# Retention and a Mish feed-forward on one core: all early loads in one order, and what their consumers need around them

## The chip, the core and the metric

The kernel runs on one core of a Trainium2 chip. A core has a matrix engine (TensorE, PE in the profile, with its weight loads as PEld), VectorE (DVE), ScalarE (ACT), GpSimd (POOL), SyncE (SP), and 16 DMA engines that move data between the device's memory (HBM) and the core's SBUF. Every engine works through its own list of instructions in order; semaphores tie the lists together. PE writes only to PSUM, from which VectorE and ScalarE read. DMA transfers are issued by SyncE, ScalarE or GpSimd, each with a queue of its own.

The metric is the time of one execution in device microseconds (us), less is better.

## The reference

Eight batches, eight heads, 576 positions, head size 64. The output of retention, heads side by side, is the input of a feed-forward layer with Mish:

```python
scores = (1/sqrt(64)) * q @ k^T
gamma  = 1 - 2 ** (-5 - h)                      # one per head h
Dmat   = gamma ** (i - j) where i >= j, else 0
x      = (scores * Dmat) @ v                     # (8*576, 512)
h      = x @ w_in                                # w_in (512, 2048)
g      = h * tanh(log(1 + exp(h)))               # Mish
out    = g @ w_out                               # w_out (2048, 512)
```

Inputs and output are float32; the kernel multiplies in bf16.

## The kernel before

**Tiles.** Positions are cut into chunks of 128 per batch (the last 64 of two batches make one chunk), 36 chunks in all, and four chunks are a tile of 512 rows: nine tiles. Tiles 0 and 1 hold the first chunk of each batch, 0 to 3 in tile 0 and 4 to 7 in tile 1. These need no state from earlier positions and have code of their own, the `f_` functions. The later tiles carry a state per batch (`state`, `step_o`). For each tile, `g1` makes one of 16 slices of h (four matmuls over w_in into the PSUM tile `hp`, then Mish by ScalarE into `gT`), and `g2` or, for tile 0, `g2_first` multiplies with w_out.

**Tiles 0 and 1.** `load_rows(queue, t, i, b)` loads q (i = 0) or k (i = 1) of one batch of tile t as float32, 256 KB, into `raw`, which lies in the two halves of a buffer (`stage`) that later is a `gT`. Tile 1's q takes the half that tile 0's k had and the other way round; tile 0's masked scores (`sm`) also lie in the half of its k. So tile 1's load of q of batch b may start only when the masked scores of batch b of tile 0 have been used by `f_out`, and its load of k when tile 0's q of that batch has been cast. `f_cast` casts to bf16, for one group of two batches or, with `one`, for one batch of it. `f_transpose` turns q and k of a group with 16 PE transposes into PSUM and copies them to `qT` and `kT`. `f_scores` makes the scores of a group (16 matmuls) and VectorE multiplies them with the decay (`sm`). `f_v` casts v of a batch; `f_out` multiplies `sm` with v and copies the result into `xT`, the input of g1.

**Order.** The program is written in the order in which each engine is to work (a manual schedule); an instruction's place among those of its engine is its place in the code. `keep_warm(n)` issues n matmuls on zeros whose result nobody reads. Tile 0's first g1 is done in two halves of the columns (`half`), the first as soon as batches 0 and 1 are ready.

**Queues.** SyncE issues six of tile 0's q and k loads and ScalarE two, before anything else (L114 to L117). GpSimd makes the constants and masks, then issues v of batches 0 and 1 (L112), then waits with a cast of v (L438) before w_in's first quarter (L439) and the v of batches 2 and 3, and so on; w_out follows at L465, then v of tile 1, then the loads of later chunks (`load`, three transfers each, and `load_k0`). Every load by GpSimd is marked by one of eight semaphores in turn, so that a load waits for the eighth before it to have landed. In g1's slices 6 and 12 of tile 0 a copy of a few values of `gT` (`passed`, L484) stands in SyncE's queue and behind it four loads of tile 1's q and k (L485), so that these are not issued before the Mish of that slice is done.

**Behind tile 0's g1** come the casts of tile 1's first group by VectorE (L487) and the 16 steps of `g2_first`; among them, by the table `steps`, tile 1's transposes (T), scores (S), casts of its second group (C), of its v (V), and its `f_out` (O). Then `g1` of tile 1 begins, with the chunks of the later tiles between its slices (`att`: P scales q, V scales v, T transposes, S scores, O output).

Of the kernel before, what the change touches and what calls it, by code (L numbers as in the profile page):

```python
# [11 lines left out]
BF16 = mybir.dt.bfloat16  # L12
AX = mybir.ActivationFunctionType
# [4 lines left out]
def kernel(  # L18
# [18 lines left out]
    nc = tc.nc  # L37
    B, H, S, D = q.shape
    assert (B, H, S, D) == (8, 8, 576, 64)
    P = 128  # L40
# [21 lines left out]
    consts = ctx.enter_context(tc.tile_pool(name="consts", bufs=1))  # L62
# [9 lines left out]
    ps_sc = ctx.enter_context(tc.tile_pool(name="ps_sc", bufs=2, space=PS))  # L72
    ps_st = ctx.enter_context(tc.tile_pool(name="ps_st", bufs=1, space=PS))
    ps_h = ctx.enter_context(tc.tile_pool(name="ps_h", bufs=2, space=PS))
    ps_o = ctx.enter_context(tc.tile_pool(name="ps_o", bufs=1, space=PS))
# [9 lines left out]
    def load_w_in(f0, n):  # L85
        nc.gpsimd.dma_start(out=w_in_t[:, :, ds(f0, n)], in_=w_in_r[:, :, ds(f0, n)])

    def load_w_out(i):
        nc.gpsimd.dma_start(out=w_out_t[:, ts(i, 4), :], in_=w_out_r[:, ts(i, 4), :])
# [11 lines left out]
    def load_rows(queue, t, i, b):  # L101
        queue.dma_start(out=raw[t][i][:, b, :],
                        in_=(q, k)[i][4 * t + b, :, 0:P, :].rearrange("h (g r) d -> g h (r d)", r=8))

    def load_second_qk(g):
        for b in (2 * g, 2 * g + 1):
            for i in range(2):
                load_rows(nc.sync, 1, i, b)

    def load_first_v(b):  # L110
        v0[b] = io.tile([P, H, D], F32, name="vraw", bufs=8)
        nc.gpsimd.dma_start(out=v0[b], in_=v[b, :, 0:P, :].rearrange("h p d -> p h d"))  # L112

    for i, b in ((0, 0), (0, 1), (0, 2), (1, 2), (0, 3), (1, 3)):  # L114
        load_rows(nc.sync, 0, i, b)
    for b in range(2):
        load_rows(nc.scalar, 0, 1, b)  # L117

# [2 lines left out]
    lnd = consts.tile([P, 1], F32)  # L121
# [6 lines left out]
    ident = consts.tile([P, P], BF16)  # L128
    make_identity(nc, ident)
    pos = consts.tile([P, 5], F32)  # L130
    nc.gpsimd.iota(pos, pattern=[[P, 5]], base=0, channel_multiplier=1,
                   allow_small_or_imprecise_dtypes=True)
    nc.gpsimd.iota(pos[64:P, 4:5], pattern=[[1, 1]], base=512, channel_multiplier=1,
                   allow_small_or_imprecise_dtypes=True)
    mask = consts.tile([P, P], F32)
    mask2 = consts.tile([P, P], F32)
    nc.gpsimd.memset(mask, 1.0)
# [16 lines left out]
    nc.scalar.activation(gq, ex, AX.Exp)  # L154
    nc.scalar.activation(gv, ex, AX.Exp, scale=-1.0)
    warm = consts.tile([P, 1], F32)

    diag = consts.tile([P, 2], F32)
    nc.vector.memset(diag, 0.0)
# [3 lines left out]
    def keep_warm(n, pool=ps_o, name="ops"):  # L163
        idle = pool.tile([P, 512], F32, name=name)
        for _ in range(n):
            nc.tensor.matmul(idle, lhsT=zeros[:, 0:P], rhs=zeros, start=True, stop=True)
# [5 lines left out]
    fst = {}  # L172
# [4 lines left out]
    def f_cast(t, i, g, copy, xs=slice(0, 2)):  # L177
        name = ("qb", "kb")[i]
        if t not in fst:
            fst[t] = {n: first.tile([P, 2, 8, 2, D], BF16, name=n) for n in ("qb", "kb")}  # L180
            fst[t]["vb"] = {}
        copy(fst[t][name][:, g, :, xs, :].rearrange("p r x d -> p x r d"),  # L182
             raw[t][i][:, ds(2 * g, 2), :][:, xs, :].rearrange("p x (r d) -> p x r d", r=8))

    def f_transpose(t, g, copies, tps):
        for i, name in enumerate(("qb", "kb")):
            for r in range(8):
                nc.tensor.transpose(tps[i][:, r, :], fst[t][name][:, g, r, :, :].rearrange("p x d -> p (x d)"),  # L188
                                    ident)
        for i, name in enumerate(("qb", "kb")):  # L190
            out_t = first.tile([P, H, P], BF16, name=name + "T", bufs=2)
            copies[i](out_t.rearrange("p h (g r) -> p h g r", r=8),
                      tps[i].rearrange("p r (g h) -> p h g r", h=H))
            fst[t][name, g] = out_t

    def f_scores(t, g):
        qT, kT = fst[t]["qb", g], fst[t]["kb", g]
# [14 lines left out]
    def f_v(t, b, copy):  # L212
        vb = first.tile([P, H, D], BF16, name="vb", bufs=4)
        copy(vb, v0[4 * t + b])
        fst[t]["vb"][b] = vb

    def f_out(t, b, copy):
        if b == 0:
            xts[t] = xp.tile([P, KC, NCH * P], BF16, name="xT")
        vb = fst[t]["vb"][b]  # L220
        if t == 0:
            pool, name = ((ps_h, "hp"), (ps_h, "hp"), (ps_st, "st"), (ps_o, "ops"))[b]
            ot = pool.tile([P, NP, P], F32, name=name)
        else:
            ot = ps_sc.tile([P, 2, NP, P], F32, name="sc")[:, 0]
        for p in range(NP):
            for e in range(2):
                nc.tensor.matmul(ot[ds(64 * e, 64), p, :], lhsT=vb[:, 2 * p + e, :],
                                 rhs=fst[t]["sm", b][:, 2 * p + e, :],
                                 start=(p == 0), stop=True, skip_group_check=True)  # L230
        copy(xts[t][:, :, ts(b, P)], ot)  # L231

    def f_state(t, b, engine=nc.gpsimd):

        n = 4 * t + b
        v0s[n] = first.tile([P, H, D], BF16, name="v0s", bufs=B)
        engine.tensor_tensor(v0s[n], v0[n], gv[:, 0, :].unsqueeze(2).to_broadcast([P, H, D]), op=OP.mult)
# [118 lines left out]
    gts = {}  # L356
    outs = {}

    def g1(t, f, cols=slice(0, NCH * P)):
        if t not in gts:  # L360
            gts[t] = gp.tile([P, nF, NCH * P], BF16, name="gT")
        hp = ps_h.tile([P, NCH * P], F32, name="hp")
        for c in range(KC):
            nc.tensor.matmul(hp[:, cols], lhsT=w_in_t[:, c, ts(f, P)], rhs=xts[t][:, c, cols],  # L364
                             start=(c == 0), stop=(c == KC - 1))
        nc.scalar.activation(gts[t][:, f, cols], hp[:, cols], AX.Mish)  # L366
# [62 lines left out]
    dve, act, pool = nc.vector.tensor_copy, nc.scalar.copy, nc.gpsimd.tensor_copy  # L429
# [1 line left out]

    half = (slice(0, 2 * P), slice(2 * P, 4 * P))
    one = (slice(0, 1), slice(1, 2))
    f_cast(0, 0, 0, dve, one[0])
    f_cast(0, 1, 0, dve, one[0])
    f_cast(0, 0, 0, dve, one[1])
    f_cast(0, 1, 0, act, one[1])
    f_v(0, 0, pool)  # L438
    load_w_in(0, 512)  # L439
    for b in (2, 3):  # L440
        load_first_v(b)
    f_v(0, 1, pool)
    for i in range(1, 4):
        load_w_in(512 * i, 512)
    keep_warm(11)
    f_transpose(0, 0, (act, dve), [ps_h.tile([P, 8, P], BF16, name="hp") for _ in range(2)])
    for i, x in ((0, 0), (0, 1), (1, 0), (1, 1)):
        f_cast(0, i, 1, act, one[x])
    keep_warm(3, ps_sc, "sc")
    f_scores(0, 0)  # L450
    f_transpose(0, 1, (act, act), [ps_st.tile([P, 8, P], BF16, name="st"), ps_o.tile([P, 8, P], BF16, name="ops")])
    f_out(0, 0, act)
    f_out(0, 1, dve)
    f_scores(0, 1)
    nc.scalar.activation(warm, pos[:, 0:1], AX.Mish)
    f_v(0, 2, pool)
    f_v(0, 3, act)
    for f in range(4):
        g1(0, f, half[0])
    f_out(0, 2, act)  # L460
    f_out(0, 3, dve)
    for f in range(4):
        g1(0, f, half[1])
    for i in range(4):
        load_w_out(i)  # L465
    for b in range(4):
        f_state(0, b)
    for b in range(4, 8):
        load_first_v(b)
    for b in range(4):  # L470
# [3 lines left out]
    nc.vector.tensor_scalar(gq, gq, 1.0 / math.sqrt(D), None, op0=OP.mult)  # L474

    passed = consts.tile([P, 2, 8], BF16)
    for f in range(4, nF):  # L480
        g1(0, f)
        if f in (6, 12):
            g = f // 6 - 1
            nc.sync.dma_start(out=passed[0:16, g, :], in_=gts[0][0:16, f, 0:8])  # L484
            load_second_qk(g)  # L485
    for i in range(2):
        f_cast(1, i, 0, dve)  # L487
    steps = {0: "T0", 3: "S0 C1", 9: "T1", 11: "S1", 12: "V0 V1 V2 V3", 14: "O0 O1", 15: "O2 O3"}
    for i in range(nF):
        for step in steps.get(i, "").split():  # L490
            n = int(step[1])
            if step[0] == "T":
                f_transpose(1, n, (dve, act), [ps_sc.tile([P, 2, 8, P], BF16, name="sc")[:, 0] for _ in range(2)])
            elif step[0] == "S":
                f_scores(1, n)
            elif step[0] == "V":
                f_v(1, n, act)
            elif step[0] == "C":
                for j in range(2):
                    f_cast(1, j, n, dve)  # L500
            else:
                f_out(1, n, (dve, act)[n % 2])
        g2_first(i // 4, i % 4)
# [13 lines left out]
    for u in range(24):  # L517
        j, w = divmod(u, 4)
# [32 lines left out]
    for t in range(2, nT + 1):  # L551
        for i in range(nF):
            n, w = NCH * (t + 1) + i // 8 * 2, i % 8
# [64 lines left out]
```

## Time and profile before

| what | value |
|---|---|
| runs, median (lowest to highest) | 324.91 us (324.73 to 325.26) |
| profiled execution | 323.0 us, of it 321.3 us span |
| PE busy | 306.2 us, 95% of the span |
| VectorE, ScalarE, GpSimd busy | 135.8, 113.6, 138.8 us |
| DMA moved | 44.42 MB, mean 138 GB/s |
| the chain that ended last | PE 88%, DMA 7% |

The span is the time from the first to the last instruction of the profiled execution; 1.7 us of that execution lie outside it. Rows of the profile name the line of the kernel, the engine, the operation, and what is written from what (`hp<-xT,w_in_t`); "idle before" is the time that the engine stood still before an instruction, and the arrow names what released it. The row of a DMA on an engine or its queue is the issue only; when the data has landed is seen from what waits for it. PE's granted clock is given for a window as a share of full speed.

Four DMA rows bear on the change: w_in's four loads by GpSimd (512 KB each) took a median of 7.6 us from issue to landing, w_out's four 15.0 us, v's 256 KB loads 5.5 us, and the eight q loads of tiles 0 and 1 by SyncE 6.6 us.

### The profile page before, as it was taken

The numbers are of one execution on the slowest core, as the hardware profiler recorded it, in microseconds if no ns is written. First come the engines' busy times: TensorE is split into PE (matmuls) and PEld (weight loads), VectorE is DVE, ScalarE is ACT, GpSimd is POOL, SyncE is SP. The second block draws the span as 40 slices with busy tenths as digits, with TensorE's granted clock in tenths as the row PEclk, the third lists the DMA queues.
The fourth block names the chain that finished last, engine by engine and source line by source line (L and its number), as shares of the span: only waits on it lengthen the run. The fifth ranks groups of instructions, "written<-read, shape, count | busy, mean of one in ns | idle before, by whom it ended". The sixth has DMA issues, their size and how long they took to land.

```text
span 321.3 us, 5751 instructions
## 1 busy us (share of the span) xinstructions
PE 306.2 (95%) x2392; PEld 155.6 (48%) x2430; DVE 135.8 (42%) x198; ACT 113.6 (35%) x186; POOL 138.8 (43%) x169
## 2 busy tenths in 40 slices
PE   6979599999999999999999999999999999999995
PEld 2654245455555545454545454545454544444444
DVE  4450145576774745453535453535354332000111
ACT  4756313566225442222222222222222222333200
POOL 5687259897736794909290808072010000000000
PEclk9999879999999999999999999999999999999999
DMA  7899999999959599898989998981434300010031
GB/s 191 186 235 197 282 303 270 223 167 177 163 106 154 104 172 218 163 153 158 156 160 107 205 139 154 141 169 46 51 82 51 83 35 33 33 35 33 33 97 68
DMA packets 73770, 44.42 MB, mean 138 GB/s; under 512 B 58768, under 2 KB 63120, under 8 KB 73744
## 3 DMA queue, kind: packets, MB, share of 16 engines
q0 software_dynamic: 46976, 25.70, 51.4%
q1 hardware_dynamic: 26336, 17.70, 25.0%
q10 hardware_dynamic: 432, 0.66, 0.8%
q8 instruction: 19, 0.31, 0.4%
q14 instruction: 7, 0.06, 0.0%
HBM read 38.80 MB, written 9.44 MB: 150 GB/s over the span
## 4 chain that ended last, share of the span: by engine, by line
PE 88%; DMA 7%; POOL 1%; issue 1%; DVE 1%; SPq 0%; ACT 0%; POOLq 0%; DVEq 0%
PE hp L364 37%; PE ops L379 29%; PE hp L379 4%; DMA vraw<-in_v_dram 4%; DMA gT<-in_k_dram 3%; PE hp L396 2%; PE sc L293 2%; PE st L325 2%; PE sc L345 2%; PE sc L350 2%; PE sc L280 1%; PE st L396 1%; PE ops L396 1%; PE hp L407 1%; PE sc L188 1%
## 5 line engine op out<-in xcount | busy, mean ns | idle before, releaser
L364 PE MATMUL hp<-xT,w_in_t 128*128 128x512 bf16 (+1 forms) x562 | 142.6, 377 | 3.3 <-DVE xT L231 0.8
L366 ACT ACTIVATE gT<-hp 128x512 bf16<-128x512 f32 (+1 forms) x148 | 86.6, 586 | 155.7 <-PE hp L364 143.5
L379 PE MATMUL ops<-w_out_t,gT 128*128 128x512 bf16 x430 | 110.1, 379 | 0.4
L364 PEld LDWEIGHTS <-w_in_t 128*128 128x128 bf16 x592 | 55.7, 99 | 63.7 <-DVE xT L231 1.3
L379 PEld LDWEIGHTS <-gT 128*128 128x128 bf16 x496 | 48.2, 98 | 58.1 <-issue 0.8
L415 DVE COPY res<-ops 128x512 f32<-128x512 f32 x28 | 19.3, 688 | 83.3 <-PE ops L379 79.6
L328 DVE TENSOR_TENSOR ssb<-st,diag 128x512 bf16<-128x512 f32 x32 | 21.9, 686 | 47.5 <-PE st L325 47.4
L255 POOL DMA_DIRECT2D qraw<-in_q_dram x24 | 22.0, 915 | 46.3 <-DVE qks L265 45.1
L271 POOL TENSOR_TENSOR vs<-vraw,gv 128x512 bf16<-128x512 f32 x28 | 29.8, 1073 | 20.4 <-issue 13.9
L297 DVE TENSOR_TENSOR sm<-sc,mask 128x1024 bf16<-128x1024 f32 x28 | 33.0, 1216 | 6.6 <-PE sc L293 6.6
L255 POOL DMA_DIRECT2D vraw<-in_v_dram x24 | 21.8, 909 | 4.6 <-DMA w_out_t<-in_moe_w_out_dram 4.0
L255 POOL DMA_DIRECT2D qks<-in_k_dram x24 | 21.9, 912 | 2.1 <-DMA w_out_t<-in_moe_w_out_dram 1.7
L265 DVE TENSOR_TENSOR qks<-qraw,gq 128x512 bf16<-128x512 f32 x28 | 18.7, 704 | 0.0
L354 DVE CAST xT<-sc 128x512 bf16<-128x512 f32 x24 | 15.4, 681 | 0.0
L379 PE MATMUL hp<-w_out_t,gT 128*128 128x512 bf16 x61 | 14.7, 379 | 0.2
L281 ACT COPY qkT<-sc 128x1024 bf16<-128x1024 bf16 x10 | 10.1, 1010 | 8.0 <-PE sc L280 8.0
L259 POOL DMA_DIRECT2D qraw<-in_q_dram x8 | 5.6, 703 | 13.8 <-DVE qks L265 13.8
L396 PEld LDWEIGHTS <-gT 128*128 128x128 bf16 x64 | 6.3, 105 | 7.7 <-issue 2.1
L182 DVE CAST qb<-gT 128x512 bf16<-128x512 f32 (+1 forms) x4 | 2.5, 619 | 17.0 <-DMA gT<-in_q_dram 17.0
L345 PE MATMUL sc<-qkT,ssb 128*64 128x128 bf16 (+1 forms) x224 | 9.5, 213 | 0.0
L350 PE MATMUL sc<-sm,vs 128*64 128x128 bf16 x192 | 9.4, 219 | 0.0
L241 POOL DMA_DIRECT2D k<-in_k_dram x8 | 7.3, 915 | 4.4 <-DMA w_out_t<-in_moe_w_out_dram 4.4
(95 smaller groups left out, 204.4 us busy)
## 6 DMA issues: line engine op xcount, KB each, us to landing
vraw<-in_v_dram POOLq DMA_DIRECT2D x32, 256.0 KB, 5.5
out_dram<-res SPq DMA_DIRECT2D x31, 256.0 KB, 2.8
qraw<-in_q_dram POOLq DMA_DIRECT2D x24, 256.0 KB, 4.1
qks<-in_k_dram POOLq DMA_DIRECT2D x24, 128.0 KB, 5.2
gT<-in_q_dram SPq DMA_DIRECT2D x8, 256.0 KB, 6.6
w_in_t<-in_moe_w_in_dram POOLq DMA_DIRECT2D x4, 512.0 KB, 7.6
w_out_t<-in_moe_w_out_dram POOLq DMA_DIRECT2D x4, 512.0 KB, 15.0
gT<-in_k_dram SPq DMA_DIRECT2D x6, 256.0 KB, 8.7
```

The lines of the kernel that those rows point to most:

```text
L255: nc.gpsimd.dma_start(out=t, in_=src[b, :, ds(P * c, P), :].rearrange("h p d -> p h d"))
L265: nc.vector.tensor_tensor(live[n]["qks"][:, 0], live[n]["q"], gq[:, c, :].unsqueeze(2).to_broadcast([P, H, D]), op=OP.mult)
L271: nc.gpsimd.tensor_tensor(vs, live[n]["v"], gv[:, c, :].unsqueeze(2).to_broadcast([P, H, D]), op=OP.mult)
L297: nc.vector.tensor_tensor(sm.rearrange("p e n i -> p (e n) i"), sc.rearrange("p e n i -> p (e n) i"), m.unsqueeze(1).to_broadcast([P, 2 * ...
L328: nc.vector.tensor_tensor(ssb.rearrange("p e n d -> p e (n d)"), st.rearrange("p n d -> p (n d)").unsqueeze(1).to_broadcast([P, 2, NP * 64 ...
L345: nc.tensor.matmul(ot[ds(64 * e, 64), p, ds(i0, iw)], lhsT=st_sb[bb, cc][:, e, p, :], rhs=qk[:, 0, p, ds(i0, iw)], start=(i0 == 0 and p == ...
L350: nc.tensor.matmul(ot[ds(64 * e, 64), p, :], lhsT=vs[:, 2 * p + e, :], rhs=sm[:, e, p, :], start=False, stop=True, skip_group_check=True)
L364: nc.tensor.matmul(hp[:, cols], lhsT=w_in_t[:, c, ts(f, P)], rhs=xts[t][:, c, cols], start=(c == 0), stop=(c == KC - 1))
L366: nc.scalar.activation(gts[t][:, f, cols], hp[:, cols], AX.Mish)
L379: nc.tensor.matmul(ops, lhsT=gts[t][:, f, ts(s, P)], rhs=w_out_t[:, f, :], start=(f == 0), stop=(f == nF - 1))
L396: nc.tensor.matmul(outs[0, s], lhsT=gts[0][:, f, ts(s, P)], rhs=w_out_t[:, f, :], start=(f == 0), stop=(f == nF - 1))
L415: copy(ot, ops)
```

## The change

Tile 0's q is loaded by SyncE, its k by ScalarE (batches 0 and 1) and by GpSimd (batches 2 and 3, ahead of the masks). GpSimd's list is put in a new order: w_in's first three quarters and v of batches 2 and 3 stand before the casts of v 0 and 1, and tile 1's q and k are issued by GpSimd between the other loads, with no copy that holds them; the two `passed` copies go. The casts of tile 0 are dealt out anew (k of batch 1 to VectorE, k of batch 2 to GpSimd, q of batch 2 to VectorE). `f_transpose` takes, for each of q and k, a list of PSUM tiles with an engine each, so that the first group goes through four half tiles in four copies, and the second through three. Mish's table is loaded by ScalarE after the three Exp, not after tile 0's scores. Two `keep_warm` of two matmuls are added, and `f_out` of batch 0 writes to another PSUM tile.

```diff
-    def load_second_qk(g):
-        for b in (2 * g, 2 * g + 1):
-            for i in range(2):
-                load_rows(nc.sync, 1, i, b)
-
...
-    for i, b in ((0, 0), (0, 1), (0, 2), (1, 2), (0, 3), (1, 3)):
-        load_rows(nc.sync, 0, i, b)
+    for b in range(4):
+        load_rows(nc.sync, 0, 0, b)
     for b in range(2):
         load_rows(nc.scalar, 0, 1, b)
...
+    for b in (2, 3):
+        load_rows(nc.gpsimd, 0, 1, b)
     mask = consts.tile([P, P], F32)
...
     warm = consts.tile([P, 1], F32)
+    nc.scalar.activation(warm, lnd, AX.Mish)
...
-    def f_transpose(t, g, copies, tps):
-        for i, name in enumerate(("qb", "kb")):
-            for r in range(8):
-                nc.tensor.transpose(tps[i][:, r, :], fst[t][name][:, g, r, :, :].rearrange("p x d -> p (x d)"),
-                                    ident)
+    def f_transpose(t, g, parts):
+
+        moves = []
         for i, name in enumerate(("qb", "kb")):
             out_t = first.tile([P, H, P], BF16, name=name + "T", bufs=2)
-            copies[i](out_t.rearrange("p h (g r) -> p h g r", r=8),
-                      tps[i].rearrange("p r (g h) -> p h g r", h=H))
+            n = 8 // len(parts[i])
+            for j, (pool, tname, copy) in enumerate(parts[i]):
+                tp = pool.tile([P, 2, 8, P] if tname == "sc" else [P, 8, P], BF16, name=tname)
+                tp = (tp[:, 0] if tname == "sc" else tp)[:, 0:n]
+                for r in range(n):
+                    nc.tensor.transpose(tp[:, r, :],
+                                        fst[t][name][:, g, n * j + r, :, :].rearrange("p x d -> p (x d)"), ident)
+                moves.append((copy, out_t.rearrange("p h (g r) -> p h g r", r=8)[:, :, :, ds(n * j, n)],
+                              tp.rearrange("p r (g h) -> p h g r", h=H)))
             fst[t][name, g] = out_t
+        for copy, to, src in moves:
+            copy(to, src)
...
-            pool, name = ((ps_h, "hp"), (ps_h, "hp"), (ps_st, "st"), (ps_o, "ops"))[b]
+            pool, name = ((ps_st, "st"), (ps_h, "hp"), (ps_st, "st"), (ps_o, "ops"))[b]
...
-    f_cast(0, 0, 0, dve, one[0])
-    f_cast(0, 1, 0, dve, one[0])
-    f_cast(0, 0, 0, dve, one[1])
-    f_cast(0, 1, 0, act, one[1])
-    f_v(0, 0, pool)
+    for b in range(2):
+        f_cast(0, 0, 0, dve, one[b])
+        f_cast(0, 1, 0, dve, one[b])
     load_w_in(0, 512)
+    f_cast(0, 1, 1, pool, one[0])
     for b in (2, 3):
         load_first_v(b)
+    for i in (1, 2):
+        load_w_in(512 * i, 512)
+    f_v(0, 0, pool)
     f_v(0, 1, pool)
-    for i in range(1, 4):
-        load_w_in(512 * i, 512)
+    load_w_in(1536, 512)
     keep_warm(11)
-    f_transpose(0, 0, (act, dve), [ps_h.tile([P, 8, P], BF16, name="hp") for _ in range(2)])
-    for i, x in ((0, 0), (0, 1), (1, 0), (1, 1)):
-        f_cast(0, i, 1, act, one[x])
+    f_transpose(0, 0, [[(ps_h, "hp", act), (ps_h, "hp", dve)], [(ps_st, "st", act), (ps_o, "ops", dve)]])
+    f_cast(0, 0, 1, dve, one[0])
+    f_cast(0, 0, 1, act, one[1])
+    f_cast(0, 1, 1, act, one[1])
     keep_warm(3, ps_sc, "sc")
     f_scores(0, 0)
-    f_transpose(0, 1, (act, act), [ps_st.tile([P, 8, P], BF16, name="st"), ps_o.tile([P, 8, P], BF16, name="ops")])
+    keep_warm(2, ps_st, "st")
+    f_transpose(0, 1, [[(ps_h, "hp", act)], [(ps_h, "hp", act), (ps_o, "ops", dve)]])
     f_out(0, 0, act)
     f_out(0, 1, dve)
     f_scores(0, 1)
-    nc.scalar.activation(warm, pos[:, 0:1], AX.Mish)
-    f_v(0, 2, pool)
     f_v(0, 3, act)
     for f in range(4):
         g1(0, f, half[0])
+    for i in range(2):
+        load_rows(nc.gpsimd, 1, i, 0)
+    f_v(0, 2, pool)
     f_out(0, 2, act)
     f_out(0, 3, dve)
+    keep_warm(2, ps_sc, "sc")
     for f in range(4):
         g1(0, f, half[1])
-    for i in range(4):
+    for i in range(2):
+        load_rows(nc.gpsimd, 1, i, 1)
+    for i in range(2):
         load_w_out(i)
-    for b in range(4):
+        f_state(0, i)
+    for b in (2, 3):
+        for i in range(2):
+            load_rows(nc.gpsimd, 1, i, b)
         f_state(0, b)
+    for i in (2, 3):
+        load_w_out(i)
     for b in range(4, 8):
         load_first_v(b)
...
-    passed = consts.tile([P, 2, 8], BF16)
     for f in range(4, nF):
         g1(0, f)
-        if f in (6, 12):
-            g = f // 6 - 1
-            nc.sync.dma_start(out=passed[0:16, g, :], in_=gts[0][0:16, f, 0:8])
-            load_second_qk(g)
...
-                f_transpose(1, n, (dve, act), [ps_sc.tile([P, 2, 8, P], BF16, name="sc")[:, 0] for _ in range(2)])
+                f_transpose(1, n, [[(ps_sc, "sc", dve)], [(ps_sc, "sc", act)]])
```

In GpSimd's list after the change the loads follow each other so: k of batches 2 and 3; v 0 and 1; w_in 0; (cast of k 2); v 2 and 3; w_in 1 and 2; (casts of v 0 and 1); w_in 3; tile 1's q and k of batch 0; (cast of v 2); q and k of batch 1; w_out 0 and 1 with the scaling of v 0 and 1 (`f_state`) after each; q and k of batch 2, q and k of batch 3, each with a scaling after; w_out 2 and 3; v 4 to 7; then the chunks as before.

## The prediction

> **What bounds the kernel now.** I read the 40 slices first: PE's digit is 9 from 40 us to the last slice, so little can be won there; the holes are in the first 40 us. Then the chain that ended last, over those 60 us (start us, length us, what):
>
> ```profile
> 3.71 7.48 DMA vraw<-in_v_dram
> ...
> 11.24 0.61 POOL vb L214
> 11.85 0.71 POOL w_in_t L86
> 12.57 0.89 POOL vraw L112
> 13.46 5.21 DMA vraw<-in_v_dram
> ...
> 18.69 0.62 ACT vb L214
> 19.31 0.29 ACT gT L366
> ...
> 30.62 8.96 DMA gT<-in_k_dram
> ```
>
> Twice the path is a load. GpSimd stands still in a cast (L214) until the first v is in, and w_in and the v of batches 2 and 3 are issued only behind that cast; ScalarE then waits for that v at 18.69, with the Mish of the first g1 behind it. Later it is tile 1's k, issued by SyncE at 30.62. PE's own order of time shows what that costs, and the windows show the clock:
>
> ```profile
> 33.68 1.46 PE L364 MATMUL hp<-xT,w_in_t 128*128 128x512 bf16 x6
> 39.06 1.04 PE L188 MATMUL sc<-ident,qb 128*128 128x128 bf16 x8 [3.92 <-DVE qb L182]
> 40.43 1.04 PE L188 MATMUL sc<-ident,kb 128*128 128x128 bf16 x8 [0.33 <-DVE kb L182]
> ...
> 51.27 0.61 PE L188 MATMUL sc<-ident,qb 128*128 128x128 bf16 x8
> ```
>
> ```profile
> 34.00:38.00 4.00, 1.14 (x6) 0.29 (x3) 0.00 (x0) 1.24 (x3) 0.55 (x1) 0.95 1.14 285
> 38.00:42.00 4.00, 2.50 (x17) 1.91 (x19) 2.52 (x3) 0.50 (x1) 0.35 (x1) 0.50 1.11 318
> 42.00:46.00 4.00, 3.89 (x26) 1.65 (x25) 0.00 (x0) 0.51 (x1) 2.64 (x3) 0.69 1.05 326
> 46.00:50.00 4.00, 4.00 (x25) 1.79 (x20) 3.81 (x4) 0.00 (x0) 3.38 (x4) 1.00 1.82 238
> ```
>
> Columns of a window: length; busy time of PE, its weight loads, DVE, ACT, POOL; then granted clock, DMA share, GB/s. After the hole PE runs at 0.50 and 0.69 of its clock, so the same eight transposes take 1.04 us at 39 us and 0.61 us at 51 us. The same view for 12 to 14 us has a DMA share of 0.25 and 9 GB/s: the DMA engines idle while the v cast holds GpSimd.
>
> **The change, part by part.**
>
> *The hold on tile 1's q and k goes* (the two `passed` copies behind g1's f = 6 and 12). The L364 row starts its six matmuls 0.216 us apart, so the next one could start at 33.68 + 6 x 0.216 = 34.98; it starts at 39.06: 4.08 us. From 39.06 to the first g1 of tile 1 (60.23) PE takes 21.17 us. At full clock the same work is 64 matmuls of g2_first at 0.216 (1.73 for 8) = 13.84, two transpose stages at 0.90 (51.27 to 52.17), two score stages at 0.55, two pairs of f_out at 0.57: 17.88 us. So the cold clock costs 3.29 us; the windows agree, 4 x 0.50 + 4 x 0.31 = 3.24. Together 7.37 us, if tile 1's data is there when g1 ends.
>
> The Trainium skill, "TensorE: Matmul & The Clock Gate" (Part 1), says that half clock lasts one window of about 3.4 us of work after an idle one, which would make an estimate of 1.7 us lost instead of 3.29, and 318.0 us in the end. The windows show the longer loss here.
>
> *Will the data be there?* Now GpSimd issues it, in one order with everything else. I add up the DMA engines' time from before's rows. q or k: before, ten 256 KB loads (8 q/k, 2 v) move from 2.3 to about 12.3 us, 1.0 us each. A half-MB piece of weights moves at 205 GB/s (20 to 28 us): 2.55 us. v alone moved at 322 to 387 GB/s (16.5 to 18 us): 0.7 us. Check: from 28.4 to 42.1 us three w_out pieces and about six q/k went through, 3 x 2.55 + 6 x 1.0 = 13.65 against 13.7 us. In the new order the engines end: first ten loads 12.4, w_in 0 at 15.0, v of 2 and 3 at 16.4, the other w_in 24.0, tile 1's q and k of batches 0 and 1 at 28.0, w_out 0 and 1 at 33.1, batches 2 and 3 at 37.1, w_out 2 and 3 at 39.7 and 42.2, v of 4 to 7 at 45.0; each lands some 0.6 us later. Tile 1's first transposes want theirs (plus two DVE casts, 0.69 each, DVE idle) at about 34: over 3 us of room. At a g1 end near 34, g2_first wants w_out 2 (i = 8) at 34 + 0.9 + 0.55 + 8 x 0.865 = 42.4 against 40.3, w_out 3 at 46.7 against 42.8, and f_out of tile 1 at 48.5, when ScalarE has cast the last v by 46.3. Room is 2 us at its tightest. Zero is charged, and this is the cover that I name: without it every us late is a us on PE.
>
> *What else is queued at GpSimd.* Ten q/k loads more than before are issued there. No such issue by GpSimd is in the trace; the nearest rows give 0.57 us (SyncE's issue of the same load) to 0.91 (GpSimd's v): I take 0.9 and keep 0.6. They stand ahead of the masks (two, 1.8 us), of f_v of batch 2 (two, which also wait for f_out of batch 0), of w_out. With them v 0 and 1 are issued at about 5 to 7 us instead of 3.7 to 5.7, w_in 0 at 7.9 instead of 12.6; the casts of v 0 and 1 end near 13.1 (14.96 before), that of v 2 near 17.4 (18.6). The first load of the later chunks' k0 goes out near 43.7 (42.7 before), all four chunks by 54; but the first transposes of chunk 8, the first after tile 1, come at about 54 (62.8 before) and its scaled v is wanted at 61. Its q and k landed long before, its v is scaled near 54.7. Nothing is charged. SyncE gives up ten issues and two holds, all of them ahead of the first store at 57.63: nothing.
>
> The Trainium skill, "SBUF — State Buffer" (two separate sides), speaks against this part: a GpSimd DMA that meets a DVE fp32 copy took 3100 ns instead of 620 there. That rule, an estimate of 2.5 us for each of ten moved issues, would put 25 us on GpSimd and make the kernel slower. Before's row where they meet is milder: the qks issue at 48.38 beside the casts of L182 took 1.24 us against 0.88, the cast 1.05 against 0.69; ten times 0.36 lies inside GpSimd's room.
>
> *The front.* Four half copies replace two whole ones (1.01 ACT, 1.22 DVE); with the 512-column rows of L231 (0.59, 0.69) as the upper and halves of the whole (0.51, 0.61) as the lower bound, the last one ends near 10.6 instead of 10.88. But three keep-warm matmuls follow the transposes (0.427 apart, to 10.7 before), so the first scores stay near 10.9, then sm 0 and 1 on DVE (1.22 each) to 14.4. Two more keep-warm matmuls (0.85) delay the second transposes to 12.8, where before they waited for k 3 until 13.39; their copies are split over ACT and DVE, kT is whole at 15.3 (15.47 before). Second scores, sm 2 and 3: end at 19.1, as before. So what lies next behind the v wait is sm 3: f_out 3 (0.39) and the xT copy (0.70) put the second half of g1 at 20.4 at best, against 22.47: 2.05 us. If PE is still at half speed in g1's first half (16 matmuls at 0.213, 16.9 to 20.3, then two f_outs at 0.65), it is 22.4: nothing won. Before turned from 1.89 to 1.47 us for eight such matmuls only at 19.65. I take 1.1, and keep 0 to 2.05. The Mish table (1.28 + 0.20 us of ACT) moves from 15.98 to 4.8, where ACT waits for the first transposes until 8.8; before it lay inside the wait for v, so it is worth nothing by itself, and 1.5 us if the v wait is gone and it had stayed.
>
> **Sum.** 7.37 + 1.1 = 8.5 us off the profiled execution's 323.0 (span 321.3 and 1.7 around it): 314.5. The runs' median is 324.91, 1.9 above the profiled one, and I take the same 8.5 off it: 316.4 us.
>
> **Rivals.**
> 1. *The tile-1 hole shrinks but w_out is late.* One queue for all means that w_out 2 and 3 stand behind eight tile-1 loads, which before came in beside them on SyncE's queue. 23.3 us of DMA work lie between v 3 and w_out 2. If it is 1.2 times that, w_out 2 lands at 45.0 and PE waits 2.6: 319.0. For it: 318 and 326 GB/s in the windows above, with both queues at work, and 205 with GpSimd's alone. Against: 205 was weights only, and v alone ran at over 320. It needs more than 1.09 times to show at all.
> 2. *The front gives the gain back.* Tile 0's k 1 goes to DVE behind q 1, k 2 to GpSimd, and v 0 starts later; if half speed stays and the copies' bounds go the bad way, the front is 0 to 1 us worse than before: 316.4 + 1.1 to 316.4 + 2.1, 318.
> 3. *Slower.* The mechanism of rival 1 from a factor of 1.4: w_out 2 lands at 49.6, PE waits 7.2 us, over the length that took the clock to half before, so 3.3 more: 10.5 against 8.5 won, 326.9. It decides from about 1.31, where PE waits 5.2 us. Nothing in the rows comes near it.
> 4. *The loads are not early after all*: GpSimd reaches tile 1's fourth load late because of the cast, the f_out waits and the landings its issues wait for. I have it at 19 us; it would have to be past 29 to matter, and each us from there is one lost; with 3 us, 319.4.
>
> **How the numbers follow.** Forecast (314.5 to 317.9) 0.72; rivals 1 and 4 together 0.13; rival 2 beyond that range 0.07; slower 0.08, with small mishaps of both kinds in it. The range of 8 in 10 goes down by the front's other 0.95 and some scatter, and up until rivals 1, 2 and 4 are mostly in: 314.6 to 319.8. Something like 0.2% (0.65 us) is what runs of this kernel can tell from no change; that takes a cancelling of 8 us, 0.02. Faster 0.91, slower 0.07.
>
> **What would show it.** Right: no gap before tile 1's L193 transposes, these at 0.61 us for eight, clock 1.00 from 30 to 50 us, g1 of tile 1 starting near 51.7, DMA busy without the hole at 12 to 14 us, w_in 0 no longer waited for. Wrong: PE waiting for w_out (rival 1), for L180's casts (rival 4), or the second half of g1 starting after 22.5 (rival 2). An unchanged clock of 0.5 after g1 would void the 3.29.

## The result, and the profile after

| | before | after |
|---|---|---|
| runs, median (lowest to highest) | 324.82 us (323.5 to 325.26) | 315.94 us (315.71 to 316.03) |
| profiled execution (span) | 323.0 us (321.3) | 315.71 us (314.0) |
| PE busy | 306.2 us | 301.0 us |

The ratio is 0.9732, with an interval of 0.9704 to 0.9761: faster by 8.9 us in the medians, by 7.3 us between the two profiled executions. The difference between these two figures is before's: its longer runs show a lower granted clock (323.17 us at a mean clock of 0.984 and 327.65 at 0.967, on one chip), and its profiled execution was a quick one. After's runs stay within 315.5 and 316.7 us on two chips.

First the chain of waits of the kernel after (start us, length us, what; "v 3" below is v of batch 3, "w_out 2" the third quarter of w_out, and so on):

```profile
2.34 6.44 DMA gT<-in_k_dram
8.84 0.68 POOL kb L180
9.52 0.86 POOL vraw L107
10.38 8.13 DMA vraw<-in_v_dram
18.53 0.62 ACT vb L219
19.15 0.29 ACT gT L371
...
34.55 0.89 PE sc L193 x16
```

Before, this stretch held three loads; the third, tile 1's k at 30.62, has left the chain. The first two are there still: GpSimd's first cast waits for k of batch 2 instead of v 0, and ScalarE's cast of v 3 starts at 18.53, where it was 18.69. Next PE in order of time, and the windows (length; busy time of PE, its weight loads, DVE, ACT, POOL; granted clock, DMA share, GB/s):

```profile
21.88 12.67 PE L369 MATMUL hp<-xT,w_in_t 128*128 128x256 bf16 x63 [0.47 <-DVE xT L236]
34.39 0.61 PE L193 MATMUL sc<-ident,qb 128*128 128x128 bf16 x8
34.83 0.61 PE L193 MATMUL sc<-ident,kb 128*128 128x128 bf16 x8
...
52.66 2.76 PE L369 MATMUL hp<-xT,w_in_t 128*128 128x512 bf16 x12
```

```profile
8.00:12.00 4.00, 2.89 (x19) 1.99 (x19) 2.83 (x5) 1.17 (x2) 3.17 (x4) 0.50 1.08 239
12.00:16.00 4.00, 3.76 (x43) 2.62 (x43) 2.91 (x4) 2.13 (x4) 2.69 (x5) 0.67 1.15 227
16.00:20.00 4.00, 2.58 (x37) 1.97 (x37) 3.37 (x4) 2.17 (x6) 3.62 (x7) 1.00 1.15 210
34.00:38.00 4.00, 4.00 (x33) 2.16 (x33) 1.22 (x1) 1.93 (x3) 1.97 (x3) 1.00 1.07 270
38.00:42.00 4.00, 3.84 (x33) 2.01 (x34) 3.38 (x4) 0.00 (x0) 2.71 (x4) 1.00 1.22 204
42.00:46.00 4.00, 4.00 (x32) 2.34 (x31) 1.40 (x2) 1.01 (x1) 1.77 (x2) 1.00 1.13 248
```

The transposes follow g1 with no gap before them, eight take 0.61 us, and the clock is 1.00 where it was 0.50 and 0.69. Before, two rows of PE in order of time that these are compared with:

```profile
22.47 12.67 PE L364 MATMUL hp<-xT,w_in_t 128*128 128x256 bf16 x63 [0.79 <-DVE xT L231]
...
60.23 2.76 PE L364 MATMUL hp<-xT,w_in_t 128*128 128x512 bf16 x11
```

Three marks divide the time. The second half of tile 0's first g1 (what lies ahead of it is called the front) starts 0.59 us earlier than before (22.47 to 21.88), from there to the transposes it takes 12.51 us instead of 16.59, and from the transposes to the first g1 of tile 1 18.27 instead of 21.17. Together that is 0.59 + 4.08 + 2.90 = 7.57 us; 0.28 of it are given back after 52.66, and 7.29 are left.

### The profile page after: what moved, and what is told of

Its sections match the earlier page's. It is cut to its first block, busy times and chain, and to the rows that moved or that the text cites. A ratio compares the mean times of both kernels' runs of the same rounds, so it can differ in the third digit from the quotient of the medians.

```text
span 314.0 us, 5760 instructions
## 1 busy us (share of the span) xinstructions
PE 301.0 (96%) x2396; PEld 153.5 (49%) x2434; DVE 137.6 (44%) x202; ACT 111.8 (36%) x184; POOL 144.6 (46%) x180
## 4 chain that ended last, share of the span: by engine, by line
PE 92%; DMA 5%; issue 1%; POOL 1%; DVE 0%; ACT 0%; POOLq 0%
PE hp L369 40%; PE ops L384 30%; PE hp L384 4%; DMA vraw<-in_v_dram 3%; PE sc L298 3%; PE st L330 3%; PE hp L401 2%; DMA gT<-in_k_dram 2%; PE sc L350 2%; PE sc L355 2%; PE sc L285 1%; PE ops L401 1%; PE hp L412 1%; PE st L401 1%; PE sc L193 1%
## 5 line engine op out<-in xcount | busy, mean ns | idle before, releaser
L384 PE MATMUL ops<-w_out_t,gT 128*128 128x512 bf16 x429 | 109.9, 379 | 0.5
L384 PEld LDWEIGHTS <-gT 128*128 128x128 bf16 x496 | 48.3, 98 | 58.0 <-issue 0.8
L276 POOL TENSOR_TENSOR vs<-vraw,gv 128x512 bf16<-128x512 f32 x28 | 29.7, 1069 | 20.4 <-issue 13.9
L260 POOL DMA_DIRECT2D vraw<-in_v_dram x24 | 21.7, 904 | 4.5 <-issue 2.8
L270 DVE TENSOR_TENSOR qks<-qraw,gq 128x512 bf16<-128x512 f32 x28 | 19.7, 734 | 1.9 <-DMA qraw<-in_q_dram 1.9
L384 PE MATMUL hp<-w_out_t,gT 128*128 128x512 bf16 x61 | 14.6, 379 | 0.3 <-issue 0.2
L298 PE MATMUL sc<-qkT 64*128 64x128 bf16 x224 | 9.0, 218 | 0.0
L401 PEld LDWEIGHTS <-gT 128*128 128x128 bf16 x64 | 5.8, 98 | 6.5
L107 POOL DMA_DIRECT2D vraw<-in_v_dram x8 | 7.3, 917 | 3.0 <-DMA w_out_t<-in_moe_w_out_dram 2.7
```

The costliest lines, as they stand in the source:

```text
L260: nc.gpsimd.dma_start(out=t, in_=src[b, :, ds(P * c, P), :].rearrange("h p d -> p h d"))
L270: nc.vector.tensor_tensor(live[n]["qks"][:, 0], live[n]["q"], gq[:, c, :].unsqueeze(2).to_broadcast([P, H, D]), op=OP.mult)
L276: nc.gpsimd.tensor_tensor(vs, live[n]["v"], gv[:, c, :].unsqueeze(2).to_broadcast([P, H, D]), op=OP.mult)
L298: nc.tensor.matmul(sc[:, e, p, :], lhsT=qk[r, 1, p, :], rhs=qk[r, 0, p, :], start=True, stop=True)
L384: nc.tensor.matmul(ops, lhsT=gts[t][:, f, ts(s, P)], rhs=w_out_t[:, f, :], start=(f == 0), stop=(f == nF - 1))
L401: nc.tensor.matmul(outs[0, s], lhsT=gts[0][:, f, ts(s, P)], rhs=w_out_t[:, f, :], start=(f == 0), stop=(f == nF - 1))
```

## The experiments

The theory at first is the prediction's: the hold made the hole and the cold clock, and v 3 sets the front. It is tried by taking parts of the change away and by doing one part alone.

### The hold and the front, each alone

Four kernels on one chip (before there: 323.3 to 330.3 us, median 327.02). *hold_off* is before without the hold, tile 1's loads still on SyncE:

```diff
     f_out(0, 0, act)
+    for i in range(2):
+        load_rows(nc.sync, 1, i, 0)
     f_out(0, 1, dve)
+    for i in range(2):
+        load_rows(nc.sync, 1, i, 1)
...
-    passed = consts.tile([P, 2, 8], BF16)
...
-        if f in (6, 12):
-            g = f // 6 - 1
-            nc.sync.dma_start(out=passed[0:16, g, :], in_=gts[0][0:16, f, 0:8])
-            load_second_qk(g)
```

The loads of batches 2 and 3 follow `f_out` of these batches in the same way.

> The kernel before, with nothing changed but the hold: tile 1's q and k of batch b are issued by SyncE right behind the f_out of batch b, without the two small copies. Theory (the hole behind tile 0's g1 and its cold clock are most of the gain, the hold alone makes them): no gap before tile 1's transposes, clock 1.00 from 30 to 50 us, 7.4 us won; the four early loads share the DMA engines with v of batches 2 and 3 and with w_in, some 1 to 2 us lost in front: 317.5 to 319.5 us. Rival (the hold was needed, and it is the single order of the loads on GpSimd that wins): the loads push v and w_in back by 4 us or more, and PE waits for w_in in g1: 321.5 us or more.

Measured: 321.43 us (320.36 to 321.84), ratio 0.9818 (0.9751 to 0.9884): between the two. PE in order of time:

```profile
25.86 4.02 PE L364 MATMUL hp<-xT,w_in_t 128*128 128x256 bf16 x17 [0.79 <-DVE xT L231]
...
40.23 0.61 PE L188 MATMUL sc<-ident,qb 128*128 128x128 bf16 x8
...
58.51 1.68 PE L364 MATMUL hp<-xT,w_in_t 128*128 128x512 bf16 x7
```

The hole is gone and the stage behind it takes 18.28 us (40.23 to 58.51), as in after. But the second half of g1 starts at 25.86 us instead of 22.47, and the windows from 16 to 28 us have a clock of 0.50. The loss is ahead of every line that was edited for the order: v 0 is there at 12.72 us instead of 11.19.

*hold_back* is after with the hold put back, tile 1's loads on SyncE behind the two copies:

```diff
-    for i in range(2):
-        load_rows(nc.gpsimd, 1, i, 0)
...
+    passed = consts.tile([P, 2, 8], BF16)
     for f in range(4, nF):
         g1(0, f)
+        if f in (6, 12):
+            g = f // 6 - 1
+            nc.sync.dma_start(out=passed[0:16, g, :], in_=gts[0][0:16, f, 0:8])
+            for b in (2 * g, 2 * g + 1):
+                for i in range(2):
+                    load_rows(nc.sync, 1, i, b)
```

> The changed kernel with tile 1's q and k taken back to SyncE's queue behind the two copies that hold them until g1's slices 6 and 12; all else as changed. Theory: the hole behind g1 is back with its cold clock, about 4 and 3 us: 322.5 to 323.8 us, tile 1's transposes at 1.04 us for eight. Rival (the order of the other loads matters more, w_out now comes earlier and the held loads find free DMA engines): the hole is under 2 us, the clock stays, 316.5 to 319 us.

Measured: 319.98 us (319.36 to 320.38), ratio 0.9779 (0.9726 to 0.9832): neither.

```profile
19.62 12.67 PE L369 MATMUL hp<-xT,w_in_t 128*128 128x256 bf16 x63 [0.47 <-DVE xT L236]
35.38 0.62 PE L193 MATMUL sc<-ident,qb 128*128 128x128 bf16 x8 [3.08 <-DVE qb L180]
36.92 0.74 PE L193 MATMUL sc<-ident,kb 128*128 128x128 bf16 x8 [0.92 <-DVE kb L180]
...
56.44 2.76 PE L369 MATMUL hp<-xT,w_in_t 128*128 128x512 bf16 x12
```

The hole came back as the theory has it: 4.00 us of idle PE, and 21.06 us from the transposes to g1 of tile 1 (0.92 of the idle time lies within these). What no theory had is the first line: the front ends at 19.62 us, 2.26 before after's, though up to there the engines' lists differ only in tile 1's first four loads, which after issues from 16.07 us on and hold_back does not. V 3 lands at 16.25 us.

*k_on_sync* gives k of batches 2 and 3 back to SyncE, and *two_tiles* makes whole-tile copies of the transposes again:

```diff
-    for b in range(4):
-        load_rows(nc.sync, 0, 0, b)
+    for i, b in ((0, 0), (0, 1), (0, 2), (1, 2), (0, 3), (1, 3)):
+        load_rows(nc.sync, 0, i, b)
...
-    for b in (2, 3):
-        load_rows(nc.gpsimd, 0, 1, b)
```

```diff
-    f_transpose(0, 0, [[(ps_h, "hp", act), (ps_h, "hp", dve)], [(ps_st, "st", act), (ps_o, "ops", dve)]])
+    f_transpose(0, 0, [[(ps_h, "hp", act)], [(ps_h, "hp", dve)]])
...
-    f_transpose(0, 1, [[(ps_h, "hp", act)], [(ps_h, "hp", act), (ps_o, "ops", dve)]])
+    f_transpose(0, 1, [[(ps_h, "hp", act)], [(ps_o, "ops", act)]])
```

> The changed kernel with k of batches 2 and 3 issued by SyncE between its q loads, as in the kernel before; GpSimd starts with v. Theory (the front's end is set by the landing of v of batch 3, which the total of the loads ahead of it sets, whoever issues them): the first transposes start at about 7.8 us, not 9.1, but v 3 lands within 0.4 us of 18.5 and g1's second half starts within 0.5 us of 21.9: 315.4 to 316.3 us. Rival (the late first transposes set the front): 1.3 us won, 314.6 us.

> The changed kernel with the first transposes in whole PSUM tiles again: q by ScalarE and k by VectorE for the first group, both by ScalarE for the second. Theory (v 3 sets the front's end, so copies ahead of it have slack): the second scores move by some 0.3 to 0.8 us and g1's second half by no more than 0.5: 315.7 to 316.5 us. Rival (the copies are on the path): 1 us lost or more, 317 us.

Measured: 315.77 us (315.66 to 316.34) and 315.81 (315.63 to 317.92); the second half of g1 starts at 21.99 and 21.79 us. Neither of these two parts of the change is worth anything here, since PE waits for the Mish behind the cast of v 3 in both (0.55 and 1.69 us): the v wait sets the front.

### Chance, or the program?

The kernels after and hold_back once more on another chip, unchanged, with two other questions beside them. *cast_later* puts the cast of v 3 on ScalarE behind the first two Mish:

```diff
-    f_v(0, 3, act)
     for f in range(4):
         g1(0, f, half[0])
+        if f == 1:
+            f_v(0, 3, act)
```

*no_warm* leaves out the two pairs of `keep_warm` matmuls that the change added.

> The changed kernel, nothing altered, beside the others on one chip: 315.7 to 316.1 us. Theory (the rate of the first loads differs from one loading of a program to the next): its DMA moves 240 to 280 GB/s between 4 and 12 us, not always the 250 of the first profile, and where it is near 275 g1's second half starts near 19.7 us instead of 21.9. Rival (the rate belongs to the program): 240 to 255 GB/s and 21.9 us again.

> The kernel with tile 1's loads taken back behind the hold, once more. Theory (rate by loading): its front may now end near 21.9 us like the changed kernel's, and it then takes 322 us, 6 us over the changed kernel. Rival (rate by program): front near 19.6 us and 320.0 us again.

> The changed kernel with ScalarE's cast of v of batch 3 put behind the Mish of g1's slices 0 and 1, nothing else. Theory (ScalarE's wait for v 3, with Mish queued behind it, ends the front; behind it comes sm 3 on VectorE, and then w_out 2 with less than 1 us of room): g1's second half starts 1.0 us earlier against the landing of v 3, and 0.3 us or so of it is given back before tile 1's f_out: 315.0 to 315.5 us. Rival 1 (the loads bound everything behind): 0.2 us or nothing. Rival 2 (nothing is given back): 314.8 us.

> The changed kernel without its two added pairs of matmuls on zeros; the eleven and the three of before stay. Theory (the clock in the front is not full before some 3 us of unbroken work, and the pairs fill holes): the clock turns full later, g1's first half runs at half speed for part of its time, 0.3 to 1.5 us lost, 316.3 to 317.5 us. Rival (v 3 hides it): 315.8 to 316.1 us.

| | time, us | GB/s, 4 to 12 us | second half of g1 starts, us |
|---|---|---|---|
| after_again | 316.36 (315.49 to 316.71) | 245 | 22.18 |
| hold_back_2 | 319.62 (319.3 to 320.87) | 271 | 19.86 |
| cast_later | 315.73 (315.64 to 316.6) | 250 | 20.75 |
| no_warm | 315.74 (315.68 to 315.82) | 246 | 21.94 |

The rates repeat (245 and 272 GB/s in their first profiles): the speed of the first loads belongs to the program, not to the run. no_warm changes nothing: the clock rises as it did, and the v wait ends last.

cast_later wins 1.13 us in the front and has none of it at the end:

```profile
20.75 12.67 PE L369 MATMUL hp<-xT,w_in_t 128*128 128x256 bf16 x63 [0.46 <-DVE xT L236]
...
42.34 1.02 PE L401 MATMUL hp<-w_out_t,gT 128*128 128x512 bf16 x4 [0.46 <-DMA w_out_t<-in_moe_w_out_dram]
...
51.38 0.41 PE L233 MATMUL sc<-sm,vb 128*64 128x128 bf16 x8 [0.27 <-ACT xT L236]
...
52.60 2.75 PE L369 MATMUL hp<-xT,w_in_t 128*128 128x512 bf16 x12
```

PE, being early, waits for w_out 2 and then for the last v of tile 1; g1 of tile 1 starts at 52.60 us against 52.66. The chain of waits now goes through w_out 2 and v 7. So in after the front and the loads bound the time almost together.

### Thirty-two bytes

Which part of a program can change the rate of loads that come before its edits? The `passed` tile is 32 bytes in each partition, among the constants, ahead of every large tile. In the compiled programs the SBUF addresses (bytes in a partition) are:

```
             before   after   hold_off  hold_back  before_shifted
w_in_t        24064   24032      24032      24064           24288
vraw         101888  101856     101856     101888          102112
gT (raw)     182784  182752     182752     182784          183008
rest by 256       0     224        224          0             224
GB/s, 4-12      267     245        238        272             241
```

Without `passed`, all targets of the early loads move from a multiple of 256 to 224 past one. The theory: a load to such a target is slower. Three kernels set the address alone, by unused bytes in the constants (32 in *aligned* and *hold_off_aligned*, which are after and hold_off; 224 in *before_shifted*):

```diff
     diag = consts.tile([P, 2], F32)
+    spare = consts.tile([P, 16], BF16)
+    nc.vector.memset(spare[:, 0:1], 0.0)
```

*aligned_cast_later* has cast_later's edit as well.

> The changed kernel with 32 bytes a partition of unused constants put where the two small copies' tile (passed) was, so that all weights, loads and results lie again at addresses that are multiples of 256, as in the kernel before; in the changed kernel they lie at 224 past one. Theory (those 32 bytes are why the same first loads moved at 240 to 255 GB/s in every kernel without the tile and at 259 to 278 in those with it): 260 to 280 GB/s from 4 to 12 us, v 3 lands near 16.4 us and g1's second half starts near 19.7, tile 1's loads land earlier too, so little is given back: 313.2 to 314.3 us. Rival (what makes hold_back's front fast is that tile 1's loads are not on GpSimd's queue): 240 to 255 GB/s and 315.7 to 316.4 us.

> The kernel before without the hold (tile 1's q and k by SyncE right behind each f_out), as in hold_off, with the 32 bytes kept that the tile of the two copies took. Theory (hold_off lost 1.5 us in front to the addresses and some more to the clock, the early loads themselves cost about 1 us): no hole behind g1, g1's second half starts near 23.5 us, 317.5 to 319.5 us. Rival (it is the early loads on SyncE's queue that push v and w_in back): as hold_off, 320.4 to 321.8 us.

> The kernel before with 224 unused bytes a partition, so that its loads go to addresses 224 past a multiple of 256, as in the changed kernel; nothing else. Theory (address): 240 to 255 GB/s from 4 to 12 us instead of 260, v 0 lands near 12.6 us instead of 11.2, the front ends 1.5 us later or more: 1.5 to 4 us slower than the kernel before on this chip. Rival (it is not the address): the same as the kernel before within its spread, v 0 at 11.2 us.

> The same 32 bytes, and ScalarE's cast of v 3 behind the Mish of slices 0 and 1. Theory (cast_later won 1.1 us in front and gave all of it back to the landing of w_out 2 and of tile 1's v; with faster loads these have room): another 0.6 to 0.9 us below aligned, 312.6 to 313.4 us. Rival (w_out and v still land last): the same as aligned within 0.3 us.

Measured on one chip (before there: 322.89 to 328.44 us, median 324.55):

| | time, us | ratio (interval) | GB/s, 4 to 12 us | second half of g1 starts, us |
|---|---|---|---|---|
| aligned | 313.58 (313.36 to 313.8) | 0.9679 (0.965 to 0.9708) | 278 | 19.54 |
| aligned_cast_later | 313.61 (312.5 to 314.13) | 0.9675 (0.9636 to 0.9715) | 280 | 20.10 |
| hold_off_aligned | 319.36 (318.62 to 320.45) | 0.9869 (0.9819 to 0.9919) | 268 | 24.13 |
| before_shifted | 332.49 and 328.02 | 1.0194 (1.0066 to 1.0322) | 241 | 25.68 |

before_shifted's four executions took 328.02, 332.49, 335.18 and 459.98 us, at mean granted clocks of 0.973, 0.958, 0.985 and 0.65. The last is the profiled one, so of its profile only the loads and GpSimd are read (its 25.68 us for PE carries no weight), and the ratio is that of the first two.

The page of after and that of aligned show the cost of the address apart from the kernel's own time (queue; packets, MB, share of 16 engines' span). After first, then aligned:

```profile
DMA packets 73066, 44.42 MB, mean 141 GB/s; under 512 B 58704, under 2 KB 63056, under 8 KB 73040
...
q0 software_dynamic: 47776, 28.32, 63.3%
q1 hardware_dynamic: 24832, 15.08, 25.9%
```

```profile
DMA packets 73066, 44.42 MB, mean 143 GB/s; under 512 B 58704, under 2 KB 63056, under 8 KB 73040
...
q0 software_dynamic: 47776, 28.32, 56.3%
q1 hardware_dynamic: 24832, 15.08, 23.5%
```

The packets and bytes are the same, but the software queue's packets took 0.633 x 314.0 = 198.8 us of the 16 engines instead of 0.563 x 311.6 = 175.4: 13% more at the shifted addresses, for the hardware queue (q1) 11%: 81.3 instead of 73.2. What that does is seen at the cast of v 3, after first, then aligned (ScalarE in order of time):

```profile
18.53 0.62 ACT L219 CAST vb<-vraw 128x512 bf16<-128x512 f32 x1 [1.53 <-DMA vraw<-in_v_dram]
```

```profile
16.19 0.62 ACT L221 CAST vb<-vraw 128x512 bf16<-128x512 f32 x1 [0.75 <-DMA vraw<-in_v_dram]
```

PE's second half of g1 in aligned:

```profile
19.54 12.67 PE L371 MATMUL hp<-xT,w_in_t 128*128 128x256 bf16 x63 [0.47 <-DVE xT L238]
```

V 3 is 2.34 us earlier, the second half of g1 starts 2.34 us earlier (21.88 to 19.54), the span is 2.4 us shorter. Nothing of that is lost behind, as cast_later's gain was, because w_out and the last v come earlier too: PE waits for neither. The engines' own operations do not change with the address: on both pages a Mish takes 586 ns and a matmul of L384 (L386 in aligned) 379. The Trainium skill, "DMA: Bandwidth & Descriptors" (How a descriptor splits into AXI transactions), has a rule that points this way: when a descriptor does not start at a multiple of 256 bytes, its first transaction starts at the multiple below, and the bytes ahead of the descriptor cost beats without being used. It tells it of reads and gives no time; here the loss shows where loads write to SBUF, and the measured 11 to 13% decide.

The loss is not spread evenly. Where v alone moves, in runs of 256 bytes, after has 213 GB/s (45 to 47 us) and aligned 348 (42 to 43 us). Where only weights move there is no loss: 206 GB/s in after (20 to 24 us), 207 in aligned (16 to 20 us). Only rests of 0 and 224 were run; what other offsets do is open.

The other direction agrees. before_shifted, whose code is before's, is slower by 1.9% in the ratio, from two runs that are 4.5 us apart. The one at a clock of 0.973 (328.02 us) is 3.5 to 4.1 us above before's runs at 0.973 and 0.974 (324.55, 324.51 and 323.96), about the upper end of what was expected; the other's clock is lower than that of any of before's runs there, so the size is not well known. In the chain of waits its v 0 is there at 12.65 us and its v 3 at 21.05, as in hold_off (12.72 and 21.24), instead of before's 11.19 and 18.67. So the address is about half of what hold_off lost in its front: aligning it brought back 1.73 of the 3.39 us there (the time is inside what was expected, at its upper end). In hold_off_aligned v 0 is there at 11.77 us, still 0.58 after before's although no edited load is issued before 15 us, v 3 is cast at 19.53, 0.84 after before's, and g1's first half runs at the half clock. Why its first loads lag is open; 0.58 us is then also what this landing can differ by between two profiles at the same addresses. The rival shows in small: PE stops in g1, for 0.59 us until 33.94, for a load of w_in.

In aligned_cast_later ScalarE no longer stands before the cast of v 3, and the chain of waits runs back to the first load of q through scores and transposes. The profiled execution is 0.56 us later than aligned at the second half of g1, and its four runs lie on both sides of aligned's. Once v is early the order of the cast is worth nothing that these runs can tell.

aligned has the time that its theory gave and beats both kernels of the case: all its runs (313.36 to 313.8) are below all of after's on two chips (315.49 to 316.71). The two did not run on one chip, but after's front repeats on its two (21.88 and 22.18 us).

## Why the prediction was right, and where its terms were off

**The hole: right.** 4.08 us were forecast and 4.08 measured. hold_back shows that the hold is the cause: with it the hole returns in after's code, without it (hold_off) it is gone from before's.

**The cold clock: right in kind, 0.39 too large.** 17.88 us were forecast from the transposes to g1 of tile 1 at full clock, 18.27 measured. Two stops of 0.16 us that the timeline puts down to "issue" ahead of two L401 groups (38.59 and 47.04 in after's chain) make 0.32 of it: a sum of rows at full speed has no place for them. The price of the hole and its clock together depends on what it meets: 6.98 us between before and after, 36.82 - 30.78 = 6.04 between hold_back and aligned, whose addresses agree; behind hold_back's hole the windows show 0.66 and then 1.00, where before's show 0.50 and 0.69. The windows' 3.24 were the better guide than the rule that the prediction weighed against them (the Trainium skill, "TensorE: Matmul & The Clock Gate", Part 1), by which 1.7 were an estimate.

**The front: the mis-sized term.** 1.1 us (0 to 2.05) were forecast and 0.59 measured. The step that failed is the one that said v 3 would be in time, so that "what lies next behind the v wait is sm 3". V 2 and 3 were to leave the DMA engines at 16.4 us and to be there about 0.6 later; the cast started at 18.53. The term that was too small is the price of a load of v: 0.7 us was forecast, and v 2 and 3 come 1.1 apart in after (their casts wait for them until 17.46 and 18.53). Both prices, this one and the 1.0 for q or k, came from before's loads, at addresses that are multiples of 256, and the diff's deletion of one small tile moved every target. With the addresses restored v 3 comes at 16.19 us and the front ends at 19.54, 2.93 before before's: more than the best that the prediction allowed (20.4), since the clock is 1.00 in g1's first half and the scores are done earlier. The copies behind the first transposes, which were to end near 10.6 us, end at 11.73 in after, as these transposes start late (9.11); but k_on_sync starts them at 8.08 and has the same front, so nothing hangs on it. Which of the front's edits makes the gain is not separated. Its sequence of the later order was right: 23.6 us lie between the landings of v 3 and w_out 2, against 23.3 forecast.

**The cover: smaller than named.** 2 us of room were forecast at w_out 2. It landed at about 42.1 us and was wanted at 42.84: 0.7. cast_later, 1.13 us earlier, waited 0.46 for it. In aligned it is 1.1 (landing at about 39.4, wanted at 40.50). V 4 to 7 were priced at 0.7 each; they came 1.2 apart, and ScalarE waited for each of them:

```profile
46.08 0.62 ACT L219 CAST vb<-vraw 128x512 bf16<-128x512 f32 x1 [0.22 <-DMA vraw<-in_v_dram]
47.28 0.62 ACT L219 CAST vb<-vraw 128x512 bf16<-128x512 f32 x1 [0.59 <-DMA vraw<-in_v_dram]
48.51 0.62 ACT L219 CAST vb<-vraw 128x512 bf16<-128x512 f32 x1 [0.60 <-DMA vraw<-in_v_dram]
49.75 0.62 ACT L219 CAST vb<-vraw 128x512 bf16<-128x512 f32 x1 [0.62 <-DMA vraw<-in_v_dram]
```

This too is the address: at aligned's 348 GB/s a load of v takes about 0.75 us, and ScalarE casts all four there without a wait. The zero charged for the data was right by a narrow margin: rival 1's mechanism was 0.7 us away, not 2.

**GpSimd's issues: cheaper than taken.** A q or k load took 0.52 to 0.60 us to issue, not 0.9, one of the ten 0.71; the lower bound was nearer. None came near the 3100 ns that the Trainium skill gives for a GpSimd DMA beside a VectorE copy ("SBUF — State Buffer", two separate sides). None of the ten issues is a step of after's chain, and k_on_sync, with two of them back on SyncE, takes the same time.

**The sum.** On the profiled execution 8.5 us were forecast and 7.3 measured. The time of 316.4 us is nearer to the measured 315.94 than that, because before's profiled execution was 1.8 us below its median and after's only 0.23 below: part of the agreement is before's scatter, that is, luck.

**The rivals.** Rival 2 (the front 0 to 1 us worse than before) is the nearest: the front came 0.59 better, half of the 1.1 forecast, and not by this rival's mechanism. two_tiles and k_on_sync show that the copies and the moved k decide nothing; what was late were the loads. Rivals 1, 3 and 4 did not occur in after.

## What to carry to other kernels

A load that is moved forward is worth the hole it leaves plus the cold clock behind the hole, if you add up the transfers in their new order and know the tightest cover; the profile before gives all three, but the price of a transfer holds for the address at which it was measured: v's 0.7 us became 1.2. When a small tile is added or deleted, compare the addresses of the tiles behind it: here 32 bytes in a partition moved all large DMA targets off a multiple of 256 and cost 2.4 us, about a quarter of what the change won, with no line of the diff that mentions addresses. If a stage ahead of an edit changes its speed, look at what the whole program shares, and set that alone in an experiment.

## What the runs showed of the hardware

- Loads to SBUF targets 224 bytes past a multiple of 256 moved 238 to 250 GB/s from 4 to 12 us, those to multiples 267 to 280, in all 14 profiles; between after and aligned, the same packets took 11 to 13% longer. Loads of v alone (runs of 256 bytes) moved 213 GB/s in after against 348 in aligned, weights alone 206 against 207.
- The granted clock of PE can stay low while PE works much of the time: in hold_off it is 0.50 in three windows of 4 us from 16 to 28 us, with PE busy 2.6 to 3.2 us in each.
- In after, a GpSimd issue of a q or k load (256 KB) took 0.52 to 0.60 us, one of ten 0.71; that of a load of v of tiles 0 and 1, of the same size, 0.92 on average.
